# Attention and a gated two-matmul block on one core: both matmuls by seven products, with Silu on ScalarE

## The chip, the cores and the metric

The kernel runs on one core of a Trainium2 chip. The metric is the device time of one execution in microseconds (us), lower is better; it is the median of several executions. A profile shows one further execution, engine by engine.

## What is computed

```python
def attention(q, k, v):                     # (8, 12, 448, 64), float32
    s = q @ k.transpose(0, 1, 3, 2) / sqrt(64)
    p = exp(s - s.max(-1)); p = p / p.sum(-1)
    return p @ v

x = attention(q, k, v).transpose(0, 2, 1, 3).reshape(3584, 768)
h = x @ w_in                                # w_in (768, 2048)
g = h * sigmoid(h)
out = g @ w_out                             # w_out (2048, 768), out (3584, 768)
```

There are 8 batches (0 to 7) of 448 tokens. The last three lines are called the block below: a first matmul, a gate (SiLU) and a second matmul.

## The kernel before

**Attention.** A batch has 12 heads, worked on in three groups of four; batch 0 is cut in two pieces of 224 tokens, so that there are 27 units (`units`). K and Q are loaded with a cast to fp16 (`load_k` L224, `load_q` L230) and turned on DVE in 32x32 blocks: `turn_k` (L279) and `turn_q` (L290) turn fp16 elements one by one into `KT` and `QT`. A score burst (`scores`, L303) multiplies four heads at once, each on 32 rows of the array; keys come in four chunks. `expo` (L340) takes two heads at a time through Exp on ACT. `attend` (L356) multiplies the exponentials with ones (part 0, the softmax sums) and with the two halves of V (parts 1 and 2), four heads side by side on 32 columns of the array each. The fourth chunk of keys is only 64 rows, so two units are paired: their fourth chunks lie in the two row halves of one buffer. DVE turns the sums, takes the reciprocal, turns them back (`inverse`, L392 to L401) and scales into the operand of the block, `xT` (`norm`, L409).

**Block.** `ffn1` (L423) makes h for 128 of the 2048 columns and 448 tokens (224 in batch 0) by six matmuls, one per 128 of the 768 inputs. `tanh` (L434, ACT) and `gate` (L470, DVE) make g = h(1+tanh h), where h is half of the real one, in `G` and `X`. The second matmul (`product`, L514) takes tiles of 128 tokens two by two (a quad): seven products of eight matmuls with 384 columns in place of eight, with sums of g made by `combine_g` (L504, DVE), sums of the weights made once (`combine_w`, L460), and the outputs put together from PSUM by three copies on ACT (L571, L577, L581) and six additions on DVE (L567). The first four tiles go plainly (`plain`, L528).

**Order.** Every engine's instructions are put in an order by a planner at build time (`Order`, `od.step`, the loop at the end). It knows a duration for each kind of instruction and picks, at every planned moment, what TensorE does next: a score burst at most every `PACE` us, otherwise work of the block, otherwise `attend`. The chip's engines then follow these fixed orders and wait for each other by semaphores. The loads with a cast stand in POOL's queue, in the order of the calls of `plan_k`, `plan_q`, `plan_v`, `plan_w_in` and `plan_w_out`; the stores are in SP's. PSUM's eight banks are two pairs for scores (`s_ring`) and four for everything else (`m_ring`). While the first loads are awaited, TensorE multiplies zeros (L1077).

Of the kernel before, what the change touches and what calls it, by code (L numbers as in the profile page):

```python
# [1 line left out]

# [13 lines left out]

SWITCH = 0.094
PE_OUT = 0.20
HOP = 0.10
DMA_RATE = 0.37  # L20
DMA_TAIL = 1.0

# [5 lines left out]
def act(n):  # L28
    return n * 0.000833 + 0.093


class Ring:
# [5 lines left out]
    def can(self, n, now):  # L38
        return len(self.free) >= n and heapq.nsmallest(n, self.free)[-1] <= now

    def when(self, n):
        return heapq.nsmallest(n, self.free)[-1] if len(self.free) >= n else None

    def take(self, n=1):
        for _ in range(n):
            heapq.heappop(self.free)

    def give(self, at):
        heapq.heappush(self.free, at)
# [13 lines left out]
class Op:  # L63


    def __init__(self, eng, busy, emit, deps=(), bias=0.0, tail=HOP, then=None):
        self.eng, self.busy, self.emit = eng, busy, emit
        self.deps, self.bias, self.tail, self.then = list(deps), bias, tail, then
        self.done = None
        self.half = False  # L70
# [5 lines left out]
class Order:  # L76


    def __init__(self):
        self.now = 0.0  # L80
        self.free = {"PE": 1.2, "ACT": 2.1, "DVE": 1.2, "POOL": 1.2}
        self.wait = {"ACT": [], "DVE": []}
        self.pool = []
        self.dma_free = 0.0
        self.out = []
        self.mode = None
        self.busy = {e: 0.0 for e in self.free}
# [8 lines left out]
    def start(self, op):  # L96
        self.emit(op.emit)
        self.free[op.eng] = self.now + op.busy
        self.busy[op.eng] += op.busy
        op.done = self.now + op.busy + op.tail  # L100
        if op.then:
            op.then(op.done)
# [7 lines left out]
    def load(self, mb, emit, ring=None, gate=None):  # L110
        op = Op("POOL", 0.58, emit)
        self.pool.append((op, mb, ring, gate))
        return op

    def step(self):

        soon = []
        for eng in ("ACT", "DVE"):
            if self.free[eng] > self.now:
                soon.append(self.free[eng])  # L120
                continue
            best = None
            for op in self.wait[eng]:
                at = op.ready()
                if at is None:
                    continue
                if at > self.now:
                    soon.append(at)
                elif best is None or at + op.bias < best[0]:
                    best = (at + op.bias, op)  # L130
            if best:
                self.wait[eng].remove(best[1])
                self.start(best[1])
                soon.append(self.free[eng])
        if self.free["POOL"] > self.now:
            soon.append(self.free["POOL"])
        elif self.pool:
            op, mb, ring, gate = self.pool[0]
            at = 0.0
            if ring is not None:  # L140
                at = ring.when(1)
            if at is not None and gate is not None:
                g = gate()
                at = None if g is None else max(at, g)
            if at is not None and at <= self.now:
                self.pool.pop(0)
                if ring is not None:
                    ring.take()
# [10 lines left out]
def kernel(  # L159
# [24 lines left out]
    NFF = DFF // 128  # L184
    NDC = DM // 128
    NT = 2 * S // 128
    OH = DM // 2
    PACE = 2.6
    LONE = NG + 1
    PIECES = ((0, 7), (7, TPP))  # L190
    NE, NXT = 9, 18
    NSG, NTMP, NOST = 3, 3, 6
# [11 lines left out]
    ones = const.tile([128, 32], FP16, name="ones")  # L204
    nc.vector.memset(ones, 1.0)
# [3 lines left out]
    w_out_t = const.tile([128, NFF, DM], FP16, name="w_out_t")  # L209

    rawk, rawq, KT, QT, VT, E, acc, rdn_t, xT, g_t, ost_t = ({} for _ in range(11))
    sT_t, inv_t = {}, {}
    pS_t = {}
# [4 lines left out]
    def load_k(b, hg):  # L222
        t = sb.tile([128, TPP, 2, 32], FP16, name=f"rk_{b}_{hg}", tag="rk", bufs=2)
        nc.gpsimd.dma_start(out=t, in_=group_of(k, b, hg))  # L224
        rawk[(b, hg)] = t

    def load_q(n):
        b, hg, g0, g1 = units[n]
        t = sb.tile([128, g1 - g0, 2, 32], FP16, name=f"rq_{n}", tag="rq", bufs=3)
# [3 lines left out]
    def form(b, hg):  # L233
        n = NG * b + hg
        return "lone" if n < LONE else ("low", "high")[(n - LONE) % 2]


    def load_v(b, hg0, hg1, x):
        if b not in VT:
            VT[b] = sb.tile([128, NH, NCH, D], FP16, name=f"V_{b}", tag="V", bufs=2)  # L240
        hs = slice(HG * hg0, HG * hg1)
        first, count = X_TOK[form(b, hg0)][x]
        nc.gpsimd.dma_start(  # L243
            out=VT[b][32 * x : 32 * (x + 1), hs, 0:count, :],
# [4 lines left out]

# [15 lines left out]
    def turn_k(b, hg, e):  # L265
        t = rawk[(b, hg)]
        if e == 0:
            KT[(b, hg)] = sb.tile(
                [128, 2, NCH, 4, 32], FP16, name=f"KT_{b}_{hg}", tag="KT", bufs=3
            )  # L270
        kt = KT[(b, hg)]
        toks = X_TOK[form(b, hg)]
        x = 0
        while x < 4:
            first, count = toks[x]
            y = x + 1
            while y < 4 and toks[y][1] == count:
                y += 1
            nc.vector.transpose(  # L279
                out=kt[:, e].rearrange("p c x i -> p x c i")[:, x:y, 0:count],  # L280
                in_=t[:, first : first + count * (y - x), e, :].rearrange(
# [5 lines left out]
    def turn_q(n):  # L287
        b, hg, g0, g1 = units[n]
        qt = sb.tile([128, 2, g1 - g0, 32], FP16, name=f"QT_{n}", tag="QT", bufs=3)
        nc.vector.transpose(out=qt.rearrange("p e g i -> p g e i"), in_=rawq[n])  # L290
        QT[n] = qt

    def score_banks(n, w, ys):
        for y in ys:
            pS_t[(n, w, y)] = ps.tile(
                [128, 2, 512], FP32, name=f"s_{n}_{w}_{y}", tag="s", bufs=2
            )

    def score(pS, n, c, e, h, x0, x1, p0):
        b, hg, g0, g1 = units[n]  # L300
        nq = 32 * (g1 - g0)
        at = nq * (c % per_burst(n))
        nc.tensor.matmul(  # L303
            out=pS[p0 : p0 + 32 * (x1 - x0), h % 2, at : at + nq],
            lhsT=KT[(b, hg)][32 * h : 32 * (h + 1), e, c, x0:x1, :],
            rhs=QT[n][32 * h : 32 * (h + 1), e],
            start=(e == 0),
            stop=(e == 1),
        )


    def per_burst(n):
        return 2 if units[n][0] == 0 else 1

    def scores(n, w, ys):
        score_banks(n, w, ys)
        for c in range(per_burst(n) * w, per_burst(n) * (w + 1)):
            for e in range(2):
                for y in ys:
                    for h in (2 * y, 2 * y + 1):  # L320
                        score(pS_t[(n, w, y)], n, c, e, h, 0, rows_of(n, c) // 32, 0)


    def scores_rest(n):
        score_banks(n, 3, (0, 1))
        for e in range(2):
            for h in range(HG):
                pS = pS_t[(n, 3, h // 2)]
                score(pS, n, 3, e, h, 0, 2, 0)
                score(pS, n + 1, 3, e, h, 2, 4, 64)  # L330

    def rows_of(n, c):
        return KROWS[c] if form(*units[n][:2]) == "lone" else 128

    def expo(n, w, y):
        kr = rows_of(n, w * per_burst(n))
        nk = 32 * (units[n][3] - units[n][2]) * per_burst(n)
        if (n, w) not in E:
            E[(n, w)] = sb.tile([128, HG, S], FP16, name=f"E_{n}_{w}", tag="E", bufs=NE)
        nc.scalar.activation(  # L340
            out=E[(n, w)][0:kr, 2 * y : 2 * y + 2, 0:nk],
            in_=pS_t[(n, w, y)][0:kr, :, 0:nk],
# [5 lines left out]
    def attend_mm(a, n, part, c, h, k0, k1, e, start, stop):  # L348
        b, hg, g0, g1 = units[n]
        nq = 32 * (g1 - g0)  # L350
        at = nq * (c % per_burst(n))
        if part == 0:
            w = ones[k0:k1, :]
        else:
            w = VT[b][k0:k1, HG * hg + h, c, 32 * (part - 1) : 32 * part]
        nc.tensor.matmul(  # L356
            out=a[32 * h : 32 * (h + 1), 0:nq],
            lhsT=w,
            rhs=e[k0:k1, h, at : at + nq],
            start=start,  # L360
            stop=stop,
        )

    def attend(ns, part):
        made = []
        lone = len(ns) == 1
        for n in ns:
            a = ps.tile([128, 512], FP32, name=f"a_{n}_{part}", tag="m", bufs=4)
            made.append(a)
            acc[(n, part)] = a  # L370
            for c in range(NCH if lone else NCH - 1):
                for h in range(HG):
                    attend_mm(
                        a, n, part, c, h, 0, rows_of(n, c), E[(n, c // per_burst(n))],
                        c == 0, lone and c == NCH - 1,
                    )
        if not lone:
            for h in range(HG):
                for i, n in enumerate(ns):
                    attend_mm(  # L380
                        made[i], n, part, 3, h, 64 * i, 64 * (i + 1), E[(ns[0], 3)],
                        False, True,
                    )

    def inverse(n, step):
        g0, g1 = units[n][2:]
        shape = [128, g1 - g0, 32]
        if step == 0:  # L390
            sT_t[n] = sb.tile(shape, FP32, name=f"sT_{n}", tag="sT", bufs=1)
            nc.vector.transpose(  # L392
                out=sT_t[n],
                in_=acc[(n, 0)][:, 0 : 32 * (g1 - g0)].rearrange("p (g i) -> p g i", i=32),
            )
        elif step == 1:
            inv_t[n] = sb.tile(shape[:2] + [1], FP32, name=f"inv_{n}", tag="inv", bufs=2)
            nc.vector.reciprocal(out=inv_t[n], in_=sT_t[n][:, :, 0:1])
# [760 lines left out]
```

The softmax here doesn't subtract the row's maximum and nothing guards it: scores larger than these inputs give would overflow.

## Time and profile before

| | |
|---|---|
| median of 3 executions | 414.13 us (413.87 to 414.46) |
| span of the profiled execution, from its first to its last instruction | 414.8 us |
| PE, matmuls | busy 402.2 us, 97% of the span, 3939 instructions |
| PE, weight loads | busy 208.0 us |
| DVE | busy 285.2 us, 69% |
| ACT | busy 233.2 us, 56% |
| POOL (its DMA issues) | busy 95.8 us, 23% |
| granted TensorE clock, mean | 0.998 |

No time of the profiled execution outside its span is given. PE's busy time counts overlapping matmuls as one stretch, so it does not say how densely the array is fed; for that one takes the spacing of matmul starts. A duration of a single DVE or ACT instruction is somewhat longer than its spacing in a run of them.

### The profile page before, as it was taken

To read this page: it belongs to the slowest core of one execution; us is meant where nothing else is said; L and a number is where in the kernel's file an instruction comes from. 1 tells how busy PE (TensorE), PEld (TensorE's weight loads), DVE (VectorE), ACT (ScalarE), POOL (GpSimd) and SP (SyncE) were. 2 spreads that over 40 slices of the span, in tenths; PEclk is the share of its full clock that TensorE was granted. 3 is DMA by queue.
4 is the path that set the end of the run, shared out by engine and by line. 5 is a ranking of instruction groups with operands and counts; after the bars stand their busy time and mean duration, and the time that the engine had idled before them with its cause. 6 is when DMAs were issued, how large, how long until landed. Compare 5 with 4: busy or idle time off the path is not lost.

```text
span 414.8 us, 9788 instructions
## 1 busy us (share of the span) xinstructions
PE 402.2 (97%) x3939; PEld 208.0 (50%) x3939; DVE 285.2 (69%) x654; ACT 233.2 (56%) x360; POOL 95.8 (23%) x175
## 2 busy tenths in 40 slices
PE   8999999899999999999999899999999999999994
PEld 8676765344454445544445444444445444555562
DVE  3556765899868477867868838949577557684763
ACT  2987884587365794058476197476683373314410
POOL 6685374723000810053100071403000000000000
PEclk9999999999999999999999999999999999999999
DMA  6999999954313960284402294365002300032014
GB/s 102 147 169 193 203 131 210 197 79 69 50 40 92 128 92 14 60 135 77 73 3 57 72 154 72 35 109 92 1 6 51 81 19 2 22 81 54 0 45 108
DMA packets 38749, 34.46 MB, mean 83 GB/s; under 512 B 11952, under 2 KB 37936, under 8 KB 38704
## 3 DMA queue, kind: packets, MB, share of 16 engines
q0 software_dynamic: 27952, 22.82, 38.2%
q1 hardware_dynamic: 10560, 10.83, 10.3%
q8 instruction: 31, 0.51, 0.5%
q10 hardware_dynamic: 192, 0.20, 0.2%
q14 instruction: 14, 0.11, 0.1%
HBM read 45.61 MB, written 11.01 MB: 136 GB/s over the span
## 4 chain that ended last, share of the span: by engine, by line
PE 79%; DMA 10%; DVE 6%; POOL 3%; issue 1%; ACT 0%; DVEq 0%
PE h L423 32%; PE p L514 27%; PE a L356 10%; PE s L303 8%; DMA rq<-in_q_dram 6%; DMA rk<-in_k_dram 3%; PE z L1077 2%; DMA w_in_t<-in_moe_w_in_dram 1%; POOL w_in_t L254 1%; DVE sT L392 1%; DVE KT L279 1%; POOL V L243 1%; DVE QT L290 1%; DVE rdn L401 1%; DVE xT L409 1%
## 5 line engine op out<-in xcount | busy, mean ns | idle before, releaser
L340 ACT ACTIVATE E<-s 128x896 f16<-128x896 f32 (+1 forms) x172 | 148.4, 914 | 54.3 <-PE s L303 53.3
L423 PE MATMUL h<-xT,w_in_t 128*128 128x448 f16 (+1 forms) x864 | 157.5, 333 | 2.5 <-DVE xT L409 1.5
L423 PEld LDWEIGHTS <-w_in_t 128*128 128x128 f16 x864 | 79.1, 98 | 75.8 <-issue 22.0
L470 DVE SCALAR_TENSOR_TENSOR G<-th,h 128x448 f16<-128x448 f16 (+2 forms) x144 | 74.9, 530 | 55.6 <-ACT th L434 52.6
L434 ACT ACTIVATE th<-h 128x448 f16<-128x448 f32 (+1 forms) x144 | 71.5, 506 | 55.6 <-PE h L423 47.3
L243 POOL DMA_DIRECT2D V<-in_v_dram x88 | 48.6, 564 | 127.6 <-PE a L356 108.5
L303 PE MATMUL s<-QT,KT 32*128 32x448 f16 (+4 forms) x864 | 54.3, 334 | 1.7 <-ACT E L340 1.1
L514 PEld LDWEIGHTS <-G 128*128 128x128 f16 x384 | 36.5, 98 | 29.3 <-issue 5.7
L514 PEld LDWEIGHTS <-S 128*128 128x128 f16 x312 | 29.3, 98 | 23.2 <-issue 4.3
L356 PE MATMUL a<-E,V 128*32 128x448 f16 (+3 forms) x864 | 40.5, 335 | 0.0
L279 DVE STREAM_TRANSPOSE KT<-rk 128x256 f16<-128x256 f16 (+2 forms) x96 | 31.6, 377 | 12.0 <-DMA rk<-in_k_dram 10.3
L514 PE MATMUL p<-D,G 128*128 128x384 f16 x208 | 37.8, 327 | 0.0
L514 PE MATMUL p<-w_out_t,S 128*128 128x384 f16 x208 | 37.0, 327 | 0.2 <-DVE S L504 0.2
L409 DVE SCALAR_TENSOR_TENSOR xT<-a,rdn 128x448 f16<-128x448 f32 (+1 forms) x54 | 28.7, 563 | 11.1 <-PE a L356 10.8
L514 PE MATMUL p<-w_out_t,G 128*128 128x384 f16 x176 | 31.8, 327 | 1.2 <-DVE m L567 1.2
L303 PEld LDWEIGHTS <-KT 32*128 32x128 f16 (+2 forms) x864 | 17.3, 98 | 28.2 <-issue 26.9
L504 DVE TENSOR_TENSOR S<-G 128x512 f16<-128x512 f16 x70 | 25.7, 416 | 5.5 <-PE p L514 5.4
L356 PEld LDWEIGHTS <-V 128*32 128x32 f16 (+2 forms) x864 | 17.9, 95 | 22.7 <-issue 14.7
L290 DVE STREAM_TRANSPOSE QT<-rq 128x896 f16<-128x896 f16 (+1 forms) x27 | 26.5, 983 | 0.1
L224 POOL DMA_DIRECT2D rk<-in_k_dram x24 | 13.6, 566 | 51.2 <-DVE KT L279 47.6
L577 ACT COPY ost<-p 128x384 f32<-128x384 f32 x13 | 6.2, 480 | 29.3 <-PE p L514 29.3
L392 DVE STREAM_TRANSPOSE sT<-a 128x448 f32<-128x448 f32 (+1 forms) x27 | 15.6, 579 | 9.6 <-PE a L356 9.6
(38 smaller groups left out, 252.0 us busy)
## 6 DMA issues: line engine op xcount, KB each, us to landing
out_dram<-ost SPq DMA_DIRECT2D x220, 48.0 KB, 1.6
rk<-in_k_dram POOLq DMA_DIRECT2D x24, 224.0 KB, 5.3
rq<-in_q_dram POOLq DMA_DIRECT2D x21, 224.0 KB, 6.0
w_out_t<-in_moe_w_out_dram POOLq DMA_DIRECT2D x8, 384.0 KB, 9.9
V<-in_v_dram POOLq DMA_DIRECT2D x43, 64.0 KB, 4.2
V<-in_v_dram POOLq DMA_DIRECT2D x40, 48.0 KB, 4.2
w_in_t<-in_moe_w_in_dram POOLq DMA_DIRECT2D x16, 96.0 KB, 4.7
w_in_t<-in_moe_w_in_dram POOLq DMA_DIRECT2D x8, 192.0 KB, 6.9
```

Source lines behind the costliest of these rows:

```text
L243: nc.gpsimd.dma_start(out=VT[b][32 * x : 32 * (x + 1), hs, 0:count, :], in_=v[b, hs].rearrange("h (i g) d -> i h g d", g=TPP)[:, :, first ...
L279: nc.vector.transpose(out=kt[:, e].rearrange("p c x i -> p x c i")[:, x:y, 0:count], in_=t[:, first : first + count * (y - x), e, :].rearr ...
L290: nc.vector.transpose(out=qt.rearrange("p e g i -> p g e i"), in_=rawq[n])
L303: nc.tensor.matmul(out=pS[p0 : p0 + 32 * (x1 - x0), h % 2, at : at + nq], lhsT=KT[(b, hg)][32 * h : 32 * (h + 1), e, c, x0:x1, :], rhs=QT[ ...
L340: nc.scalar.activation(out=E[(n, w)][0:kr, 2 * y : 2 * y + 2, 0:nk], in_=pS_t[(n, w, y)][0:kr, :, 0:nk], func=AF.Exp, scale=attn_scale,)
L356: nc.tensor.matmul(out=a[32 * h : 32 * (h + 1), 0:nq], lhsT=w, rhs=e[k0:k1, h, at : at + nq], start=start, stop=stop,)
L409: nc.vector.scalar_tensor_tensor(out=xT[(b, cc)][:, 32 * g0 : 32 * g1], in0=acc[(n, part)][:, 0:nq], scalar=0.5, in1=rdn_t[n].rearrange("p ...
L423: nc.tensor.matmul(out=h[:, 0 : t1 - t0], lhsT=w_in_t[:, cc, 128 * f : 128 * (f + 1)], rhs=xT[(b, cc)][:, t0:t1], start=(cc == 0), stop=(c ...
L434: nc.scalar.activation(out=th, in_=h_t[(b, f, t0)][:, 0 : t1 - t0], func=AF.Tanh)
L470: nc.vector.scalar_tensor_tensor(out=dst[:, f, at + lo : at + hi], in0=th_t[(b, f, t0)][:, lo - t0 : hi - t0], scalar=1.0, in1=h_t[(b, f, ...
L504: nc.vector.tensor_tensor(out=dst[:, f0:f1], in0=x[:, f0:f1], in1=y[:, f0:f1], op=op)
L514: nc.tensor.matmul(out=pr_t[(qd, BANK[m])][:, 0:OH], lhsT=w[:, f, :], rhs=W_[m][:, f, :], start=(f == 0 and BANK[m] == m), stop=(f == HF - 1),
```

## The change

- **First matmul, batches 2 to 7** (`Fold`): the eight block products (2 halves of tokens by 2 halves of the inputs by 2 halves of the outputs) become seven, of three matmuls with 224 columns each. Four sums of `xT` per batch (`plan_t`) and four of `w_in` (`plan_w_in_sums`) are made before; after the fifth step a copy of two partial results to SBUF (ACT or DVE), then four additions from PSUM on DVE (y, c22, c12, c21) and a subtraction on POOL (z).
- **Gate, batches 2 to 7**: one Silu on ACT writes `G` directly, in place of Tanh and DVE's multiply-add. [...] No score burst is planned while more than four Silus of a batch are open (`silu_phase`).
- **Second matmul** (`Quad`): a form of seven products that shares sums: four sums of g in place of five, two copies and one more on ACT or DVE, four additions on DVE. All 14 quads go this way, `plain` is gone. Half of the sums may be put on POOL.
- **K and Q** are turned as 32-bit pairs: half the elements on DVE, and the operands of the scores are then read with a step of two elements.
- **Exponentials**: the first two chunks of a unit are added (DVE or POOL), and part 0 multiplies three chunks with ones in place of four. The paired fourth chunk is read with zeros in the other half of V (set by POOL) or of ones, so that every unit multiplies four whole chunks.
- **Loads**: `w_out` is moved in POOL's queue from batch 1 to just before batch 3's K; V has one buffer in place of two, Q two in place of three.
- **PSUM**: the score banks may be lent to the block while no score is planned.

The core of the diff, cut:

```diff
-    PACE = 2.6
+    PACE = 2.3
+    SUMS, EKEEP, ESENG = (0, 1), 2, 'VP'
+    QB = 4
+    LIM_H = 3
+    PLAIN = 2
+    SILU = 2
+    W_OUT_AT = NG * len(PIECES) + 6
...
-        nc.vector.transpose(out=qt.rearrange("p e g i -> p g e i"), in_=rawq[n])
+        nc.vector.transpose(
+            out=qt.rearrange("p (g i) e -> p g (i e)", i=32).bitcast(FP32),
+            in_=rawq[n].bitcast(FP32),
+        )
...
-            rhs=QT[n][32 * h : 32 * (h + 1), e],
+            rhs=QT[m][32 * h : 32 * (h + 1), :, e],
...
+        if part == 0 and sums:
+            chunks = [sums[0]] + chunks
...
+    def silu(out, src):
+        nc.scalar.activation(out=out, in_=src, func=AF.Silu, scale=2.0)
...
+    class Fold:
+        ORDER = (1, 5, 2, 6, 7, 3, 4)
+            lhs = {
+                1: WI[0, 0], 2: WI[0, 1], 3: SI[4], 4: WI[1, 1], 5: SI[1], 6: SI[2], 7: WI[1, 0],
+            }[m]
...
+            if m == 5:
+                ev["copy"] = od.add(
+                    Op(
+                        "ANY", {"ACT": act(2 * n), "DVE": vec(2 * n)},
+                        lambda e: copy(e, F[:, 0:2], src), [op], SLOW,
+                    )
+                )
+            elif m == 6:
+                add("y", "DVE", y, A[:, n : 2 * n], p1, ALU.add, [op])
+                add("z", ZENG, p5, y, p5, ALU.subtract, [ev["y"]])
+            elif m == 3:
+                c12 = add("c12", "DVE", A[:, n : 2 * n], A[:, n : 2 * n], p1, ALU.add, [op])
+                self.finish(A[:, 0 : 2 * n], self.f, [c12], True)
+            elif m == 4:
+                c21 = add("c21", "DVE", p5, Bq, p5, ALU.add, [op, ev["z"]], lambda at: banks.give(k, at))
+                self.finish(F[:, 1:3].rearrange("p i n -> p (i n)"), self.f + HF, [c21], False)
+            if m in (6, 7) and self.at >= 5 and "c22" not in ev:
+                add("c22", "DVE", y, Bq, y, ALU.add, [self.last7, ev["y"]] + [ev["z"]])
...
+        o1 = sums(T_s[:, 0], x[0, 1], x[0, 0], ops[0])
+        o2 = sums(T_s[:, 1], x[1, 1], T_s[:, 0], [o1] + ops[1])
+        o4 = sums(T_s[:, 2], x[1, 0], T_s[:, 1], [o2])
+        o3 = sums(x[0, 1], x[1, 1], x[0, 1], [o1] + ops[1])
...
+        if b >= PLAIN:
+            moe += [Fold(b, f) for f in range(HF)]
```

## The prediction

> **What bounds the kernel now.** First the page's head, for the engines and for what the span looks like in 40 slices (tenths busy, 10.4 us each):
>
> ```profile
> PE 402.2 (97%) x3939; PEld 208.0 (50%) x3939; DVE 285.2 (69%) x654; ACT 233.2 (56%) x360; POOL 95.8 (23%) x175
> ...
> PE   8999999899999999999999899999999999999994
> DVE  3556765899868477867868838949577557684763
> ACT  2987884587365794058476197476683373314410
> ...
> DMA  6999999954313960284402294365002300032014
> ```
>
> PE is busy throughout; DVE and ACT are not full anywhere for long; the DMA engines are full for the first 80 us only. A busy PE need not be a fed PE, so next the waits that name PE, of all waits:
>
> ```profile
> PE h L423 <- DVE xT L409: 1.5, 2, 1.2
> PE p L514 <- DVE m L567: 1.2, 1, 1.2
> PE s L303 <- ACT E L340: 1.1, 3, 0.4
> ```
>
> These are its longest (besides 1.0 us for the zeros); after the first 25 us the matmuls wait for almost nothing. Third the timeline of PE, which prices a matmul by the distance of starts:
>
> ```profile
> 45.38 1.90 PE L423 MATMUL h<-xT,w_in_t 128*128 128x224 f16 x18
> 47.21 0.94 PE L356 MATMUL a<-E,ones 128*32 128x448 f16 x16
> 48.08 0.56 PE L303 MATMUL s<-QT,KT 32*128 32x448 f16 x8
> 48.57 2.47 PE L423 MATMUL h<-xT,w_in_t 128*128 128x224 f16 x24
> 50.98 0.56 PE L303 MATMUL s<-QT,KT 32*128 32x448 f16 x8
> ...
> 96.56 2.44 PE L423 MATMUL h<-xT,w_in_t 128*128 128x448 f16 x12
> 98.94 0.56 PE L303 MATMUL s<-QT,KT 32*128 32x448 f16 x8
> 99.43 3.58 PE L423 MATMUL h<-xT,w_in_t 128*128 128x448 f16 x18
> 102.94 1.63 PE L356 MATMUL a<-E,V 128*32 128x448 f16 x32
> 104.50 2.44 PE L423 MATMUL h<-xT,w_in_t 128*128 128x448 f16 x12
> ```
>
> 18 matmuls of 448 columns take 3.51 (99.43 to 102.94), 12 take 2.38: 0.188 us each. 24 of 224 columns take 2.41, 18 take 1.83: 0.097 us each, so half the columns cost half the time and the weight load (0.098 us a piece, beside it) does not show. 16 of 384 columns take 2.60 (0.1625 each) in the last stage. A score burst is 0.49, its eight matmuls, four abreast, 0.38 of that: a change between full, row and column tiling costs about 0.11.
>
> The counts times these prices: first matmul 672 x 0.188 + 192 x 0.097 = 144.9; second 792 x 0.1625 = 128.7; scores 32.6; `attend` some 49. That is 355 of 414.8 us. The rest: some 18 before the block starts (the loads), 30 for tiling changes, 6 after the last matmul, 5 of waits. **TensorE's stream of columns is the bound**, so columns saved are time saved as long as its suppliers keep up.
>
> [...]
>
> **The change, part by part, on PE.**
> - First matmul: 6 batches x 8 folds x 21 = 1008 matmuls of 224 columns x 0.097 = 97.8; batches 0 and 1 are as before, 18.6 + 96 x 0.188 = 18.0. Sum 134.4 against 144.9: **-10.5**.
> - Second: 14 x 56 = 784 against 792 matmuls: **-1.3**.
> - `attend`: a pair of units now takes 3 x 1.56 = 4.68 with an entry each, 4.35 without. After: V 2 x 2 x 16 matmuls, 4 abreast, = 16 x 0.188, ones 2 x 12 = 6 x 0.188, sum 4.14: -0.2 a pair, ten pairs, **-2.1**. The instruction order of the changed kernel shows 19 of 21 units with the sum. It has 253 changes of tiling against 241: **+1.3**.
> - Zeros and start: K and Q are turned faster before the first scores; the order has 12 zero matmuls fewer ahead of them: **-0.7**, but the loads set the pace from there, so I count -0.5.
>
> Sum -13.1. With nothing else late the span would be **401.7**.
>
> **The other engines.** Rows used:
>
> ```profile
> L434 ACT ACTIVATE th<-h 128x448 f16<-128x448 f32 x112 | 61.2, 546 | 53.6 <-PE h L423 45.6 <-DVE xT L409 4.5 <-ACT th L434 2.9
> L409 DVE SCALAR_TENSOR_TENSOR xT<-a,rdn 128x224 f16<-128x224 f32 x12 | 4.6, 385 | 5.2 <-PE a L356 5.1
> L392 DVE STREAM_TRANSPOSE sT<-a 128x448 f32<-128x448 f32 x21 | 13.2, 628 | 7.6 <-PE a L356 7.6
> L340 ACT ACT_TABLE_LOAD x1 | 1.3, 1283 | 0.7 <-PEq L1143 0.7
> ```
>
> - DVE loses 80 gates' worth (74.9 to some 24: -51) and half of the turns (58.1 to 34, a 448-element 32-bit turn at 0.63: -24); it gains 192 fold additions at 0.385 (+74), some copies (+7), 24 sums of `xT` (672 elements at the rate of L504's 512 in 0.42: 0.5, +12), 20 sums of exponentials (+12); quads and weights about even. 285 becomes some **314**.
> - ACT: Tanh 71.5 to 20.4, Silu at the Tanh row's 0.546: 80 whole and 16 cut in two, +55; more copies, +11; 11 more table loads, +14 [...]. 233 becomes **263** [...].
> - POOL gains some 48 subtractions of 224, 18 sums of 896, 60 others of 384 to 768 elements. The trace has no row. [...]
> - Over 402 us each still has room. So outside the folds I cost them at nothing: there the scores, quads and `attend` leave PE the cover that it has now (82 to 294 us before: ACT busy at most 67%, DVE at most 83% of a stage).
>
> **Where the cover is gone: the folds.** The order of the changed kernel has almost bare runs of some 95 to 165 fold matmuls, once per batch. A batch's folds take PE 168 x 0.097 = 16.3 us. In them ACT does 8 x (copy 0.546 + two Silus 1.09) = 13.1 and two table loads 2.6 = **15.7**; DVE 8 x 1.54 + 2.0 for the sums = **14.3**[...]. (Runs of instructions overlap: five Exps of 0.915 took 4.14, 9% less; that helps both.) What was a stage of one engine at its limit has three near it. A fold is also a chain: two steps, copy, two steps, y, z on POOL, c22, last step, c21, Silu. [...] POOL's z stands behind DMA issues only outside these runs, by the order. Value taken: **0.5 us of PE waiting per batch, +3** (the 9% of overlap gives ACT and DVE some 1.3 us a batch); bounds 0 (the overlap suffices) and 0.6 us a fold, +29 [...].
>
> Elsewhere, waits that the change adds:
> - After the last fold, TensorE's last quads wait for its additions and Silu (some 1.5 us by the rows); before, two tiles were ready: **+1**, bounds 0 and 3.
> - Batch 1's first matmul no longer has 64 plain matmuls (10.4 us) ahead of it, but its K, Q and V come ahead of `w_out`'s first half, 8 issues of 384 KB in all, 9.9 us from issue to landing each, and so earlier: taken as even, bounds -1 and +4. V's single buffer delays loads that are awaited much later: hidden by the K and Q already there.
> - Lock of DVE and POOL: [...] **+1**, bounds 0 and 6.
> - The scores' stepped operands: **0**, upper bound 32 if the reading halved.
>
> Sum: 414.8 - 13.1 + 3 + 1 + 1 = 406.7. The runs' median stands 0.7 below the profiled span: **406**.
>
> **The rivals.**
> - *Everything is hidden* (the overlap of instructions keeps ACT and DVE ahead): 401.7 + 1 - 0.7 = 402, down to 397 if fewer waits than now remain. For it: DVE and ACT have more slack over the whole than the sums need.
> - *The folds become bound by ACT, DVE and POOL in turn* (slower): at 0.6 us of waiting a fold, 48 folds, 401.7 + 29 + 2 - 0.7 = 432. It decides against the change from 13.1/48 = 0.27 us a fold, against 0.06 assumed. For it: 15.7 and 14.3 of 16.3. Against it: Silu and the copy do not depend on each other across folds.
> - *The stepped operands cost* (slower): from half of the scores' 32.6 us at a third more time, together with the waits assumed, no gain is left; at double, 441. [...]
> - *Waits eat all of it*, within 0.2% (0.8 us, about what a measurement of this kernel tells from no change): 414.
>
> **How the numbers follow.** Forecast (403 to 411) 0.44; all hidden (396 to 403) 0.22; no change 0.05; folds bound 0.24, most of it at 416 to 428; operands 0.05. Faster 0.66, same 0.05, slower 0.29. The range 395 to 425 leaves out the worst of the two slower cases and little below; the likeliest case alone is 403 to 411.
>
> **What would show it.** Right: some 1008 matmuls of 224 columns at 0.097 us spacing; score bursts still 0.49 us; in fold runs PE waits of half a microsecond or so a batch on DVE or ACT; DVE near 310, ACT near 265 busy. Wrong: spacing of the fold matmuls above 0.11, or PE waits on the additions, copies and Silus of the folds summing to over 13 us; a score burst of 0.7; PE idle between 50 and 80 us on `xT`.

## The result and the profile after

The changed kernel takes **505.75 us** (median of 4 runs, 505.42 to 506.33) where the kernel before takes 414.29 (413.87 to 415.91): a ratio of 1.2185, 95% interval 1.2124 to 1.2245. The profiled execution has a span of 503.6 us against 414.8, **88.8 us** more. Each ratio in this document is taken against runs of the kernel before made alongside, without those of either kernel in which the clock was low and the same kernel took longer (the kernel before beside e12: 420.14 to 423.58 us at a clock of 0.969 to 0.976, against 413.9 to 418.66 at 0.987 to 0.999). The page of the changed kernel, engines and slices (tenths busy, now 12.6 us each):

```profile
PE 418.7 (83%) x4281; PEld 251.6 (50%) x4281; DVE 324.4 (64%) x701; ACT 262.3 (52%) x405; POOL 238.8 (47%) x321
...
PE   8998867996669889798888888889888798887874
DVE  2456778759796755674587535877684776665651
...
POOL 5566979976576612553255432444342423212320
PEclk9799999999799999999999999999999999999999
```

TensorE (PE) is no longer busy throughout, from the first slices to the last, so no single stage is at fault. No other engine is full either: DVE is at 64% of the span and ACT at 52%. Something makes engines wait in turn. The waits of PE, those largest in total (us in total, times, longest):

```profile
PE p L485 <- DVE t L454: 7.3, 2, 6.5
PE p L804 <- DVE xT L465: 6.3, 10, 1.4
PE p L804 <- DVE t L510: 6.3, 8, 2.6
PE p L920 <- ACT G L506: 5.9, 10, 1.8
PE p L485 <- DVE G L501: 5.2, 6, 2.7
```

L485 is the plain first matmul, L804 the second matmul, L920 the folds. The PE waits that the timeline shows (those of over 0.15 us) sum to 78.8 us in 133 places; before they sum to 6.7 us in 12. The second line is the odd one. **The second matmul reads `w_out` and g; the scaling of attention's output into `xT` (L465) gives it nothing. Yet it waited ten times for that.** One place in PE's timeline (start, duration, and in brackets the idle time before it and what ended it):

```profile
271.26 0.50 PE L804 MATMUL p<-w_out_t,G 128*128 128x384 f16 x2
272.48 0.48 PE L804 MATMUL p<-w_out_t,G 128*128 128x384 f16 x2 [0.72 <-DVE xT L465]
```

What the two have in common is PSUM, the memory that matmuls write their results to. In the kernel before, each bank of the block and of `attend` is a tensor of its own. In the changed kernel all eight banks are four tensors of two, so that score banks can be lent:

```python
P_s = [ps.tile([128, 2, 512], FP32, name=f"p_{i}") for i in range(4)]
def bank(i):
    return P_s[i // 2][:, i % 2]
```

In the built programs the waits between engines are made for whole tensors. A matmul that writes bank 1 of a pair is made to wait until DVE has read bank 0, and a read of bank 0 until the matmuls into bank 1 are done. Counted in the program, some 240 of TensorE's waits (some 165 for DVE, 70 for ACT) are for an instruction that touches only the neighbouring bank, and over a hundred waits of DVE and ACT for TensorE are of the same kind; in the kernel before there is none. Laid beside the trace, matmul by matmul, 108 of the 133 waits and 64.6 of the 78.8 us end at such an instruction, all ten waits of the second matmul for `xT` among them. The planner books single banks and does not know of these waits.

A second thing shows on DVE. Its timeline and POOL's around the longest PE wait, at 122.9 to 129.5 us:

```profile
122.52 4.93 DVE L510 TENSOR_TENSOR xT<-xT,xT 128x672 f16<-128x672 f16 x1
127.37 0.49 DVE L510 TENSOR_TENSOR T<-xT,T 128x672 f16<-128x672 f16 x1
...
122.18 1.65 POOL L329 DMA_DIRECT2D V<-in_v_dram  x3
123.84 3.23 POOL L510 TENSOR_TENSOR TO<-w_out_t 128x768 f16<-128x768 f16 x2
```

A sum of `xT` that takes 0.5 us elsewhere took 4.93 beside POOL's issues and two of its sums; it ended 0.4 us after them. TensorE's wait of 6.54 us ends at a DVE instruction further back in the same queue, and one that reads only the neighbouring bank: here both losses meet. The first 1.3 us of the sum lie beside DMA issues alone; what held it there is not shown, since beside the same issues without POOL's sums (e6) 12 sums of 672 elements took 0.488 to 0.507 us. POOL is held up as well, by less: its sums of 512 elements take 1.16 us in the median and up to 1.56, DVE's with both operands in SBUF 0.42 and up to 2.09, and every one of POOL's above 1.16 and of DVE's above 0.43 runs beside a sum of the other.

### The profile page after: what moved, and what is told of

It reads as the page before. It is cut to its first block, busy times and chain, and to the rows that moved or that the text cites. A ratio compares the mean times of both kernels' runs of the same rounds, so it can differ in the third digit from the quotient of the medians.

```text
span 503.6 us, 10883 instructions
## 1 busy us (share of the span) xinstructions
PE 418.7 (83%) x4281; PEld 251.6 (50%) x4281; DVE 324.4 (64%) x701; ACT 262.3 (52%) x405; POOL 238.8 (47%) x321
## 3 DMA queue, kind: packets, MB, share of 16 engines
q0 software_dynamic: 27952, 22.82, 32.7%
## 4 chain that ended last, share of the span: by engine, by line
PE 36%; DVE 18%; ACT 6%; issue 3%; DMA 1%; POOL 0%; ACTq 0%; DVEq 0%; SPq 0%; POOLq 0%
PE p L804 15%; PE p L920 14%; PE p L432 5%; DVE E L510 5%; ACT G L506 3%; DVE p L510 3%; DVE t L510 2%; DVE S L510 2%; PE p L383 2%; DVE xT L465 2%; ACT E L514 1%; DVE t L516 1%; DVE t L454 1%; DMA out_dram<-t 1%; ACT L506 1%
## 5 line engine op out<-in xcount | busy, mean ns | idle before, releaser
L408 ACT ACTIVATE E<-p 128x896 f16<-128x896 f32 (+1 forms) x172 | 149.0, 915 | 81.6 <-PE p L383 79.7
L920 PEld LDWEIGHTS <-w_in_t 128*128 128x128 f16 x576 | 55.7, 98 | 30.5 <-issue 27.1
L920 PE MATMUL p<-xT,w_in_t 128*128 128x224 f16 x432 | 61.7, 260 | 9.9 <-DVE p L510 3.3
L804 PE MATMUL p<-w_out_t,G 128*128 128x384 f16 x304 | 59.3, 326 | 8.9 <-DVE xT L465 3.0
L804 PEld LDWEIGHTS <-G 128*128 128x128 f16 x416 | 38.8, 97 | 49.0 <-issue 27.8
L510 DVE TENSOR_TENSOR E<-p,E 128x224 f32<-128x224 f32 x108 | 40.6, 387 | 32.2 <-PE p L920 25.7
L485 PE MATMUL p<-xT,w_in_t 128*128 128x224 f16 (+1 forms) x288 | 45.7, 294 | 17.9 <-DVE t L454 7.3
L383 PE MATMUL p<-QT,KT 32*128 32x448 f16 (+4 forms) x864 | 57.2, 346 | 2.6 <-ACT E L408 2.2
L510 POOL TENSOR_TENSOR E<-E,E 128x896 f16<-128x896 f16 x18 | 35.6, 1976 | 44.6 <-ACT E L408 44.5
L804 PE MATMUL p<-TO,S 128*128 128x384 f16 x208 | 41.7, 326 | 10.3 <-DVE p L510 2.3
L804 PEld LDWEIGHTS <-S 128*128 128x128 f16 x312 | 28.4, 97 | 43.2 <-issue 23.8
L920 PE MATMUL p<-T,SI 128*128 128x224 f16 x288 | 43.8, 261 | 4.3 <-ACT G L506 2.3
L920 PEld LDWEIGHTS <-SI 128*128 128x128 f16 x432 | 41.7, 98 | 9.6 <-issue 8.6
L432 PE MATMUL p<-E,V 128*32 128x448 f16 (+2 forms) x864 | 44.1, 338 | 2.4 <-DVE G L501 0.9
L514 ACT COPY t<-p 128x384 f32<-128x384 f32 x24 | 11.5, 479 | 65.9 <-PE p L804 39.1
L485 PEld LDWEIGHTS <-w_in_t 128*128 128x128 f16 x288 | 26.2, 98 | 38.6 <-issue 31.6
L465 DVE SCALAR_TENSOR_TENSOR xT<-p,t 128x448 f16<-128x448 f32 (+1 forms) x54 | 30.0, 567 | 24.0 <-PE p L432 17.8
```

The source lines that it names most:

```text
L383: nc.tensor.matmul(out=P_s[s_pair][p0 : p0 + 32 * (x1 - x0), h % 2, at : at + nq], lhsT=KT[(b, hg)][32 * h : 32 * (h + 1), c, x0:x1, :, e] ...
L408: nc.scalar.activation(out=E_s[e_i][0:kr, 2 * y : 2 * y + 2, 0:nk], in_=P_s[s_pair][0:kr, :, 0:nk], func=AF.Exp, scale=attn_scale,)
L432: nc.tensor.matmul(out=bank(a)[32 * h : 32 * (h + 1), 0:nq], lhsT=w, rhs=E_s[sum_at[n] if part == 0 and c in sums else es[c // per_burst(n)]][
L465: nc.vector.scalar_tensor_tensor(out=x_s[xi][:, cc % HC, 32 * g0 : 32 * g1], in0=bank(a)[:, 0:nq], scalar=0.5, in1=t_s[ti][:, 0:nq], op0=A ...
L485: nc.tensor.matmul(out=bank(a)[:, 0 : t1 - t0], lhsT=w_in_t[:, cc, 128 * f : 128 * (f + 1)], rhs=x_s[x_at[(b, cc // HC)]][:, cc % HC, t0:t ...
L510: e.tensor_tensor(out=out, in0=a, in1=b, op=op)
```

## The experiments

Theory 1 puts the loss on DVE and POOL excluding each other, that is on the hold-ups just shown, theory 2 on the folds; the stepped operands are tried apart, and theory 3, the paired banks, came after the first four runs. In e5 and e8 every engine's instructions stand in the same order as in the kernel that they start from. In the others the planner makes the order anew, and part of a difference can come from the order itself.

**e1: no arithmetic on POOL.** All sums that POOL made go to DVE.

```diff
-    SUMS, EKEEP, ESENG = (0, 1), 2, 'VP'
+    SUMS, EKEEP, ESENG = (0, 1), 2, 'DVE'
...
-    HIGH = 'POOL'
-    ZENG = 'POOL'
+    HIGH = 'DVE'
+    ZENG = 'DVE'
...
-    VPS = (3, 4)
-    WENG = 'VP'
+    VPS = ()
+    WENG = 'DVE'
```

> The changed kernel with all its arithmetic on POOL moved to DVE (sums of exponentials, the folds' z, half of the sums of g, the sums of the weights); the loads and the zeroing of V stay on POOL. Theory 1 ([...] the fixed orders pass each hold-up on): the 35 us or so by which DVE's two-input instructions are stretched go, and with them most of TensorE's 81 us of waits, although DVE gets some 50 us more to do: 420 to 450 us. Theory 2 (the folds with three engines near their limit are the loss): DVE is fuller than before, so no gain: 490 to 520 us.

Measured 491.69 us (491.2 to 492.18), ratio 1.1848 [1.179, 1.1907]. POOL's busy time falls from 238.8 to 100.9 us and PE's waits only from 79 to 65. Theory 1 gives 14 us of 91 at most: not the main cause.

**e2: no sums of exponentials**, `SUMS = (0, 9)`, so part 0 multiplies four chunks again.

> The changed kernel without the added exponentials: part 0 multiplies all four chunks with ones again. Theory 1 (mutual exclusion): the longest POOL instructions (18 of 1.98 us) and 20 of DVE's stretched ones go, TensorE gets 19 x 4 matmuls four abreast, 3.6 us, more: 480 to 495 us. Theory 2 (the folds are the loss): about 3 us more work, nothing else: 500 to 510 us.

Measured 523.42 us (523.07 to 523.78), ratio 1.2613 [1.2551, 1.2675]: slower by 18 us than with them, outside both ranges. Taking work off POOL and DVE made it worse, which no theory of a loaded engine explains. The matmuls that return are 3.6 us of it; most of the rest is 12 us more of PE's waits in the new order (90.6 us, of which at least 67 end at a neighbouring bank). With the banks apart the same edit costs 3 us (e11 against e5, below).

**e3: no folds**, `PLAIN = 8`: the first matmul as before in all batches.

> The changed kernel with the plain first matmul in all batches, and so Tanh and the DVE gate; the new second matmul, the exponentials' sums, the 32-bit turns and POOL's other arithmetic stay. Theory 1 (mutual exclusion): POOL keeps its sums of g and of exponentials, loses the z, so part of the loss stays although TensorE has 10.5 us more to do: 460 to 490 us. Theory 2 (the folds are the loss): 415 to 440 us.

Measured 526.62 us (526.5 to 526.75), ratio 1.269 [1.2629, 1.2751]. The folds are not the loss: without them it is 21 us more, of which 10.5 are the columns that they save and 11.5 more waits of PE. The waits largest in total (us, times, longest) are many small ones, of the plain first matmul (L485) and of the second (L804):

```profile
PE p L485 <- ACT th L498: 18.1, 27, 1.0
PE p L804 <- DVE t L510: 13.8, 16, 2.2
PE p L485 <- DVE G L501: 10.4, 21, 2.7
```

**e4: the kernel before with the 32-bit turns of K and Q alone**, and so with the stepped operands in the scores.

```diff
-        nc.vector.transpose(out=qt.rearrange("p e g i -> p g e i"), in_=rawq[n])
+        nc.vector.transpose(
+            out=qt.rearrange("p (g i) e -> p g (i e)", i=32).bitcast(FP32),
+            in_=rawq[n].bitcast(FP32),
+        )
...
-            rhs=QT[n][32 * h : 32 * (h + 1), e],
+            rhs=QT[n][32 * h : 32 * (h + 1), :, e],
```

> The kernel before with one part of the change alone: K and Q turned as 32-bit pairs, scores reading with a step of two elements, loads and everything else as before (the planner is given the shorter turns). If stepped operands are free and DVE is not the bound: within 1% below before, 410 to 414.5 us, DVE busy some 24 us less. If the stepped operands cost, score bursts of eight matmuls go above 0.49 us and the time above 420 us.

Measured 413.82 us (412.75 to 417.7), ratio 0.998 [0.9945, 1.0015]. DVE is busy 264.3 us, 21 less than before, and the time does not change by an amount that can be told. The stepped operands cost little by the trace: an undisturbed score burst takes 0.507 us from its start to the next matmul's (median of 63 in e4; 0.507 in the changed kernel too), against 0.490 before. One of e4's:

```profile
133.62 0.57 PE L306 MATMUL s<-QT,KT 32*128 32x448 f16 x8
134.13 2.44 PE L426 MATMUL h<-xT,w_in_t 128*128 128x448 f16 x12
```

The 0.017 us are some 2 us over the 108 bursts (an estimate from these numbers), too little to be told in the total.

**e5: banks as tensors of their own.** The one edit to the changed kernel is the layout of PSUM: two pairs for scores, four single banks.

```diff
-    P_s = [ps.tile([128, 2, 512], FP32, name=f"p_{i}") for i in range(4)]
+    P_s = [ps.tile([128, 2, 512], FP32, name=f"p_{i}") for i in range(2)]
+    M_s = [ps.tile([128, 512], FP32, name=f"m_{i}") for i in range(4)]
...
-        return P_s[i // 2][:, i % 2]
+        return P_s[i // 2][:, i % 2] if i < 4 else M_s[i - 4][:, :]
```

> The changed kernel with one edit: PSUM banks 4 to 7, which the block and attend use, are four tensors of one bank in place of two tensors of two banks; order, instructions and sizes stay. Theory 3 (two banks in one tensor: 239 of TensorE's waits on DVE and ACT are for an instruction that uses only the neighbour bank, and as many as 100 waits of DVE and ACT on TensorE likewise; the planner books single banks and knows nothing of it): TensorE's waits fall from 81 us to below 20, time 400 to 425 us. Theory 1 (DVE and POOL exclude each other): 35 us of stretched DVE instructions stay, time above 470 us. Theory 2 (the folds): unchanged, 500 us or more.

Measured 444.51 us (443.29 to 446.34), ratio 1.0701 [1.0636, 1.0766]: **61 us of the 91 come back from this edit alone**, more than from any other. TensorE's waits for a neighbouring bank fall from some 240 to 18 in the program and from 64.6 to 1.2 us in the trace, and all its waits from 78.8 to 32.7 us. The second matmul no longer waits for `xT`; the waits that lead now:

```profile
PE m L486 <- DVE X L502: 5.9, 1, 5.9
PE m L805 <- DVE t L511: 5.2, 5, 2.2
PE m L805 <- DVE S L511: 3.2, 5, 1.1
PE m L486 <- DVE G L502: 3.2, 1, 3.2
```

The expectation was too low, for the time and for the waits: those for other reasons grew from 14 to 31.5 us, and a second cost is left.

**e6: e5 and e1 together** (single banks, no arithmetic on POOL).

> The kernel of e5 with POOL's arithmetic moved to DVE as in e1. If, once the banks are apart, the exclusion of DVE and POOL is the next loss: 5 to 15 us below e5. If DVE's load counts more (it gets some 50 us more to do, less the 35 us of stretching): 5 to 25 us above e5.

Measured 428.48 us (427.54 to 429.42), ratio 1.0301 [1.0221, 1.0381]: 16 us more come back, one more than the top of what was expected; PE's waits fall from 32.7 to 21.5 us. DVE's sums in the changed kernel and in e6, by kind (ns, shortest/median/longest; first and last start); first the changed kernel:

```profile
L510 DVE TENSOR_TENSOR E<-p,E x108: 379/391/393, 185.6 to 475.4; 128x224 f32<-128x224 f32 x108
L510 DVE TENSOR_TENSOR S<-S,G x22: 360/418/2085, 78.8 to 479.7; 128x512 f16<-128x512 f16 x22
L510 DVE TENSOR_TENSOR E<-E,E x20: 602/672/2303, 42.5 to 442.7; 128x896 f16<-128x896 f16 x20
```

Then e6:

```profile
L511 DVE TENSOR_TENSOR S<-S,G x22: 405/415/424, 66.2 to 406.7; 128x512 f16<-128x512 f16 x22
L511 DVE TENSOR_TENSOR E<-E,E x38: 581/615/626, 40.6 to 377.0; 128x896 f16<-128x896 f16 x38
```

With POOL free of arithmetic the longest of these is within 3% of the median; with it, up to five times the median. The additions with one operand in PSUM (first line, 379 to 393 ns) are never stretched. The sum of `xT` above (4.93 us) and one in e11 below (6.41) were held for longer than one of POOL's sums beside them lasts (1.64 and 0.87 us).

**e7: e5 without folds**, `PLAIN = 8`.

> The kernel of e5 with the plain first matmul, Tanh and DVE's gate in all batches, as in e3. TensorE has 10.5 us more to stream, DVE and ACT less to do. If the folds pay what their columns save: 5 to 12 us above e5. If their waits eat it: within 3 us of e5 or below it.

Measured 447.78 us (444.92 to 450.65), ratio 1.0765 [1.0653, 1.0877]. Against e5 the folds bring 3 us where their columns save 10.5, and the ranges touch, so their worth here is hardly shown.

**e8: the kernel before with paired banks.** Its four single banks become two pairs, used in a fixed turn; every instruction stays, at `h`, `p`, `o` and the zeros as at `a`. The fixed turn lets some partial results of the second matmul be overwritten before their last use.

```diff
+    P_m = [ps.tile([128, 2, 512], FP32, name=f"pm_{i}") for i in range(2)]
...
+        i = m_next["i"] % 4
+        m_next["i"] += 1
+        return P_m[i // 2][:, i % 2]
...
-            a = ps.tile([128, 512], FP32, name=f"a_{n}_{part}", tag="m", bufs=4)
+            a = m_bank()
```

> The kernel before with one edit: its four single PSUM banks for the block and attend are two tensors of two banks, used in turn; nothing else changes. Theory 3: TensorE waits for readers of the neighbour bank here too; 102 of its waits on DVE and 48 of those on ACT are of that kind: 440 to 500 us. Theories 1 and 2, which lie in what the change adds: 413 to 417 us.

Measured 457.95 us (455.99 to 459.92), ratio 1.101 [1.0913, 1.1107]. The layout costs some 43 us in the kernel before as well, inside theory 3's range, with none of the change's arithmetic in it. Part of it may be the fixed turn: of 28.1 us of PE's waits, 16 to 18 end at a neighbouring bank. Two of its new waits (us, times, longest), of the first matmul for the gate and of the second for its additions:

```profile
PE pm L431 <- DVE G L478: 4.4, 11, 0.8
PE pm L522 <- DVE m L575: 3.7, 5, 1.8
```

**e9, e11: an order that knows the exclusion.** e11 is e5 without the sums of exponentials. e9 is e11 with a planner that means to put no DVE sum of two SBUF operands beside POOL's arithmetic. ("The first kernel" of e11's text and "the previous kernel" of e10's are e9.)

```diff
+        self.lock = isinstance(busy, dict) and eng != "ANY"
...
+        if op.lock:
+            self.lock = self.now + busy
...
+                    if op.lock:
+                        at = max(at, self.lock)
```

> Separate single-bank tensors as in the bank experiment; besides, the planner that writes the orders now knows that a DVE addition with two SBUF inputs and an addition on POOL exclude each other, so it puts neither beside the other; the sums of exponentials are not made. Theory 'the rest of the loss (444.5 down to 428.5 without POOL arithmetic) is the exclusion that the order does not know of': an order that knows it gives back most of it, 408 to 422 us; TensorE waits 15 us or less, no DVE addition of two SBUF operands stretched beyond 1.5 us. Rival 'the rest is the density of work of the folds, whatever the order': 428 to 445, DVE stretched as little, TensorE waiting as in the bank experiment (33 us).

> The bank experiment's kernel without the sums of exponentials, the planner not knowing of the exclusion: the pair to the first kernel of this call. Exclusion theory: 422 to 440 us, that is 10 or more above the order that knows the exclusion, with DVE additions stretched by POOL's. Rival (the sums of exponentials themselves, POOL's longest instructions, were all of the exclusion's cost): within 3 us of the first kernel.

Measured: e9 434.59 us (433.24 to 436.79), ratio 1.041 [1.0346, 1.0475]; e11 447.45 (446.73 to 450.66), ratio 1.0725 [1.0651, 1.0798]. The order is worth 13 us, as the exclusion theory said, but e9 is 13 above the top of what that theory expected and inside the rival's range; its waits are 21.8 us where 15 at most were expected, and a DVE sum is still stretched to 2.21 us. Against the rival, by which the order does not matter, stands e11. There one sum of the weights on DVE, of 0.35 us elsewhere, took 6.41 while seven of POOL's in a row ran from start to end, and TensorE's longest wait, 5.1 us, follows it:

```profile
54.54 6.41 DVE L511 TENSOR_TENSOR SI<-SI,w_in_t 128x384 f16<-128x384 f16 x1
...
52.88 6.11 POOL L511 TENSOR_TENSOR SI<-SI,w_in_t 128x384 f16<-128x384 f16 x7
```

In e9 the longest wait of PE is 6.2 us, at 58 us. DVE's and POOL's timelines there:

```profile
58.11 1.76 POOL L519 TENSOR_TENSOR SI<-w_in_t 128x384 f16<-128x384 f16 x2
59.84 0.90 POOL L519 TENSOR_TENSOR SI<-SI,w_in_t 128x384 f16<-128x384 f16 x1
...
59.91 1.43 DVE L519 TENSOR_TENSOR SI<-SI,w_in_t 128x384 f16<-128x384 f16 x1 [4.42 <-POOL SI L519]
61.25 2.71 DVE L519 TENSOR_TENSOR SI<-w_in_t,SI 128x384 f16<-128x384 f16 x2
63.89 0.97 DVE L510 SCALAR_TENSOR_TENSOR G<-th,m 128x224 f16<-128x224 f16 x3
```

A sum of the weights stands on DVE and waits 4.42 us for one on POOL, which came to its sums only at 51.1 us, after V's loads. The first fold begins at 161 us, so nobody needs these sums yet; but behind them in DVE's queue stand the gates that TensorE waits for.

**e10: e9's planner with the sums of exponentials**, the weight sums all on DVE.

> As the previous kernel with the sums of exponentials kept (part 0 multiplies three chunks), the sums of the weights all on DVE. Exclusion theory: 412 to 425 us, TensorE's waits 10 to 20. Rival (density): 430 to 445. Against the previous kernel it shows what the sums of exponentials are worth once the order accounts for their cost on POOL: up to 4 us less by the matmuls saved, or more by their time on DVE and POOL.

Measured 440.21 us (438.61 to 442.35), ratio 1.0543 [1.0476, 1.061]. It is 5.6 us slower than e9, outside the exclusion theory's range and inside the rival's. Whether the sums of exponentials cost more on DVE and POOL than the matmuls they save is not settled by it: the weight sums moved as well, and between e5 and e11, which differ by the sums of exponentials and the order that follows, the kernel with them is 3 us faster.

**e12: e9 with the weight sums on DVE** and one of g's four sums on POOL in place of two.

```diff
-    PACE = 2.3
+    PACE = 2.2
...
-    VPS = (3, 4)
-    WENG = 'VP'
+    VPS = (3,)
+    WENG = 'DVE'
```

> The kernel that plans with the exclusion and makes no sums of exponentials, with the sums of the weights on DVE alone and one of the four sums of g on POOL in place of two (score bursts at most every 2.2 us). In e9 TensorE's longest wait, 6.2 us at 58 us, is behind a sum of the weights on DVE that waits for one on POOL. Theory 'what is left of the loss are waits that POOL's sums bring': no wait of TensorE over 3 us between 50 and 80 us, waits of 12 to 17 us in all, 415 to 428 us; the before kernel is not beaten by more than 0.5%. Rival 'what is left is the clock granted and the density of matmuls, not POOL': 430 to 437, the granted clock 0.97 to 0.98 as before.

Measured 423.35 us (422.47 to 423.89), ratio 1.0191 [1.0154, 1.0228]: the fastest of the versions with folds, 82 us below the changed kernel and still some 2% above the kernel before. PE's waits sum to 14.2 us, the longest 1.5. Time and waits lie where the theory of POOL's sums put them; what each of the three edits gave is not shown. Its page:

```profile
PE 402.7 (96%) x4357; PEld 252.2 (60%) x4357; DVE 293.2 (70%) x720; ACT 258.7 (61%) x403; POOL 160.7 (38%) x266
...
PE   8999998999999999999989999999999899999895
```

No run beat both kernels; e4 is level with the kernel before.

## Why the prediction was wrong

**The 88.8 us, added up.** PE's idle time before matmuls, with the gaps too short for the timeline's brackets, grew by 74 us (81.0 - 6.9). A matmul that is followed by another overlaps with it: the starts of three of 224 columns and of the next three are 0.29 us apart, while the three, counted to their end (which the profile models), take 0.45:

```profile
189.19 0.45 PE L920 MATMUL p<-xT,SI 128*128 128x224 f16 x3
189.47 0.45 PE L920 MATMUL p<-xT,w_in_t 128*128 128x224 f16 x3
```

So at every wait 0.16 us of tail, otherwise covered, stands open and counts as busy: 121 waits more, some +19. The granted clock, 0.981 against 0.998, is +7 at most; the scores' steps are +2; the columns saved are -13.1; the end after the last matmul is 1.9 shorter. Together +87. The idle time is read off; tails, clock and steps are estimates from these numbers.

By the steps of the prediction:
- **Columns, prices, tiling (-13.1): right in kind.** The folds run at 0.096 us a matmul, the score burst at 0.51, and there are 252 changes of tiling in the trace where 253 were counted. PE is busier by 16.5 us rather than less: tails, clock and steps make up most of it, by the estimate above.
- **Stepped operands (0): nearly right.** The 0 was the author's assumption; the trace before did not show it. By e4 some 2 us, not told in the total. (Two sums of that rival are off: at double cost it is 406 + 32.6 = 439, not 441, and a third more on half of the scores is 5 us, which leaves some of the gain.)
- **Engine loads: near.** ACT 262.3 against 263; DVE 324.4 against 314, with stretched sums in it. POOL is busy 238.8 us, for whose arithmetic the trace before had no row. ACT's table load, 1.28 us, came 12 times, six times ahead of an Exp and six ahead of a Silu; where nothing else was waited for (ten of them), ACT's next instruction began 11 or 12 ns after it.
- **Folds, 0.5 us a batch (+3): right as a term of its own, hidden in the result.** PE idled 22.1 us before fold matmuls in the changed kernel, over the 13 named as the sign of a wrong forecast. With single banks (e5) it is 2.9, or 0.48 a batch; in e12 it is 6.0, or 1 a batch, so that e5 comes so near the 0.5 is in part luck. The slower rival, ACT, DVE and POOL bound in turn inside the folds (its 0.6 us a fold was an estimate that no trace showed), is not what happened: e3 is slower still without folds.
- **Lock of DVE and POOL (+1, bounds 0 and 6): mis-sized.** e5 to e6 is 16 us (11 of them waits of PE), outside the bounds; e1, with the banks still paired, gives 14. The term was the author's estimate: POOL did no arithmetic in the trace before, so nothing there showed it. And DVE works through its instructions in the planned order: gates and turns that TensorE needs stand behind a stretched sum (one was stretched by 4.4 us) or a waiting one, as in e9, where TensorE waited 6.2 us.
- **The step that failed: "as long as its suppliers keep up".** It was tested for busy time, stage by stage and in the folds, and the list "Elsewhere, waits that the change adds" was made from the order of instructions. The line on PSUM in the change ("the score banks may be lent") has no term in the sum: it was put at nothing, without a look at what the new tensors make each instruction wait for. That is 61 us (e5), the largest term: with the banks apart PE's idle time falls by 47 us and its busy time, the tails above all, by 15. It could have been counted before any run: some 240 waits for the bank next door. It lay outside every rival, which is why the range missed too. The rival nearest in number, 432, has another cause, the folds.
- **Loads of batch 1 (-1 to +4) and the last fold (0 to 3)** were not tried alone.

**What stays open.** e12's span is 6.8 us above that of before. Its columns save 9.5 (3.6 us of matmuls return without the sums of exponentials), its waits cost 7.5 more and their tails 3, and the scores' steps 2. The granted clock in its first 40 us was some 0.83 (0.984 over the span), which would be 6 by estimate; but runs of it at 0.990 to 0.996 took as long (spans of 420.7 to 422.1). Where those last us lie was not found. Nor was it found why e6, without arithmetic on POOL, is still some 3% above the kernel before, with 15 us more of PE's waits.

## What to carry to other kernels

Before pricing the arithmetic of a change, compare what each instruction waits for in both programs: in these programs two banks put into one tensor made their users wait for each other (61 us, e5), and a planner that booked them apart could not see it. An engine that is busy for 97% of the span leaves 3% for all waits for its suppliers, so work moved off it pays only if these waits do not grow by as much. When POOL takes over additions, plan it and DVE's additions of two SBUF operands as one resource (here worth 13 us, e11 against e9), or keep POOL to DMA issues (16 us, e5 against e6).

## What was not expected of the hardware

- A DVE addition with both operands in SBUF was stretched from 0.50 to 4.93 us beside POOL: that one ended 0.4 us after the second of two POOL sums in a row, so it was not let in between them, and in e11 one of 0.35 us took 6.41 through seven in a row. With an operand in PSUM none was stretched (108 additions between 379 and 393 ns).
- POOL took 0.66 us for a subtraction of 224 fp32 elements and 1.98 for a sum of 896 fp16 elements; the trace before had no row for either.
- A wait of TensorE cost more here than the idle time that the profile shows: by the spacing of starts (0.29 us for three matmuls that take 0.45 to their end) some 0.16 us more, the end of a matmul that the next one otherwise covers.
- Score operands read with a step of two fp16 elements were not quite free: 0.507 us a burst against 0.490.
